# Running the conv units of a conv-plus-spectral-mix kernel from the last row blocks to the first

## The chip, the cores and the metric

The kernel runs on one core of a Trainium2 chip. The core has a matrix engine (TensorE, PE in the profile; PEld is its loading of stationary operands), a vector engine (DVE), a scalar engine (ACT), a general engine (POOL) that also issues DMAs, and a sync engine (SP) that only issues DMAs. Sixteen DMA engines move data between the device memory and the on-chip memory. The metric is the device time of one execution in microseconds (us); lower is better. Before the change the median of three runs is 177.28 us (176.27 to 177.85).

## What is computed

The input `x` is 8 batches of 3264 rows of 192 channels. First comes a causal convolution over rows with 7 taps: the 192 channels belong to 8 heads of 24, and each head has its own softmax-normalised taps. On its result `u` stands a spectral mix: the first 64 Fourier modes along the rows are taken, each mode is multiplied by its own complex 192x192 matrix, and the result is transformed back. Last comes `out = v + relu(v @ w_ch)` with `v = u + mixed`.

```python
w = softmax(weight)                       # (heads, 7)
u = einsum('hk,bskhg->bshg', w, windows(x, 7))
X = rfft(u, axis=1)[:, :64]
Y = einsum('bmd,mde->bme', X, w_r + 1j * w_i)
v = u + irfft(Y, n=S, axis=1)
out = v + maximum(v @ w_ch, 0)
```

## The kernel before

**Rows and blocks.** The rows of a batch are cut into 13 blocks of 256 rows; the last has 192. A block is held in `xall` as two halves of up to 128 rows, in bf16. Batches go in pairs: `q` is the pair (0 to 3), `i` the batch in the pair. The DMA that loads `x` casts it from four bytes to two.

**Units.** The conv stage runs over `units`: a unit is a pair and a run of blocks `(q, t0, n)`. Pair 0 has the units (0,2), (2,3), (5,4), (9,4), the other pairs (0,5), (5,4), (9,4), so there are 13 units, in rising order of blocks (L44 to L46). For each unit the four calls of `conv_group` (L295) handle two heads each. A head and a parity of the output row (`e`) have up to five products: two of the half blocks with the near part of the band matrix (L307), one for the rows that the second half of the block before gives (L312, all blocks of the unit but its first), one for those that the first half gives the second (L315), and, in units that don't begin at block 0, one of 48 columns for the first block of the unit (L319). The conv result is written over its input in `xall` (L326 on ACT for groups 0 and 2, L328 on DVE for 1 and 3), so the raw last rows of a unit are kept in a tile `side` for the next one: `keep_side` (L330) copies them on DVE (L334) before the unit starts. The products go to three PSUM tiles in turn (`zc`), so a fourth group waits until the first has been copied out.

**Fourier sums.** `dft_unit` (L336) multiplies the finished blocks of a unit with the table `ftab` and adds them up over the 13 blocks of a pair in one PSUM bank (L342). The map `after` (L376) says behind which group of which unit that is issued, one unit later in most cases. At the end of a pair the sums are copied out (L346) and `xtrans` turns them by six products a batch (L355, L357).

**The table.** `ftab` holds cosines and sines for 26 half blocks. `table_dve` (L194) computes the angles on DVE in four instructions (L198, L202, L203, L205), `table_act` (L209) the sine, the absolute value and the cosine on ACT (L213, L215, L217). Two pieces are made, half blocks 0 to 10 (`TA`) and 10 to 26; their steps are put between conv groups by the map `between` (L368).

**Loads.** All loads of `x` and of the weights are issued from POOL in program order, so that every instruction on POOL stands in one queue with them. `load_rows` (L139) loads the blocks of one batch of a unit; `load_last` (L150) loads the last block, one batch of all pairs at a time and each half by itself. The first loads of `x` have 2 and 3 blocks. Behind those of `x` come the channel matrix (L273 to L275) and the mode matrices, two loads for a group of four modes (`load_w`, L277), 16 groups in seven slots; `load_free` (L284) issues a load as soon as the group that used the slot before it has been mixed.

**Mix.** When the conv stage is over, PE alternates 12 products of a group (`mix`, L461, products L468) with transposes of `xall` and of the table (L417, L427) that the last stage needs. `mix_copy` and `mix_trans` (L474, L477) copy the products of two groups and turn them by four transposes (L481) into a bf16 PSUM tile, from which `yet_copy` (L485) copies on DVE and ACT (L491, L493). The last two groups have a path of their own (L606 to L617, transposes L608). Then the mixed modes are scaled (L435) and 52 items of the last stage (`z_c`, `z_g`, products L504) give the output, which SP stores.

The order of instructions is that in which the program writes them; each engine runs its own in that order. What is run when is thus set by hand, by `between`, `after` and the place of the loads.

Of the kernel before, what the change touches and what calls it, by code (L numbers as in the profile page):

```python
# [17 lines left out]
def kernel(  # L18
# [72 lines left out]
    side = [sb(f"side{i}", [2, D], BF16) for i in range(2)]  # L91
# [58 lines left out]
    def load_last(h):  # L150
        r = P if h == 0 else 64
        for i in range(2):
            src = bass.AP(tensor=x.tensor, offset=x.offset + (i * S + 256 * (NB - 1) + P * h) * D,
                          ap=[[D, r], [2 * S * D, NQ], [1, D]])
            nc.gpsimd.dma_start(out=xall[0:r, :, NB - 1, h, i, :], in_=src)
# [7 lines left out]
    load_rows(units[0][0], 0, *units[0][1:])  # L163
# [3 lines left out]
    load_rows(units[0][0], 1, *units[0][1:])  # L167
    load_unit(*units[1])
# [3 lines left out]
                   allow_small_or_imprecise_dtypes=True)  # L172
    load_unit(*units[2])
    load_unit(*units[3])
# [3 lines left out]
    nc.vector.memset(bandyet[:], 0.0)  # L178
    nc.vector.memset(halfpi[:], math.pi / 2)
# [56 lines left out]
    nc.vector.memset(xall[64:P, :, NB - 1, 1, :, :], 0.0)  # L236
# [26 lines left out]
    for u in units[4:7]:  # L263
        load_unit(*u)
# [6 lines left out]
    for u in units[7:]:  # L271
        load_unit(*u)
# [22 lines left out]
    def conv_group(k, g):  # L295
        q, t0, n = units[k]
        zt = zc[seq[0] % 3]
        seq[0] += 1
        sd = side[k % 2]
        for hd in range(2):  # L300
            h = 2 * g + hd
            dsl = slice(GRP * h, GRP * h + GRP)
            cols = zt[:, hd, 0:96 * n].rearrange("p (t e c) -> p t e c", t=n, e=2)
            for e in range(2):
                for half in range(2):
                    r = slice(64 * half, 64 * half + 64)
                    nc.tensor.matmul(cols[r, :, e, :].rearrange("p t (i d) -> p t i d", i=2),  # L307
                                     band[:, e, h, 0:64], xall[:, q, t0:t0 + n, half, :, dsl],
                                     start=(e == 0), stop=False, tile_position=(0, 64 * half),
                                     skip_group_check=True)  # L310
# [13 lines left out]
        srcv = zt[:, :, 0:96 * n].rearrange("p k (c d) -> p k c d", d=GRP)  # L324
        if g % 2 == 0:
            nc.scalar.copy(out=dst, in_=srcv)  # L326
        else:
            nc.vector.tensor_copy(out=dst, in_=srcv)  # L328

    def keep_side(k):  # L330
        q, t0, n = units[k]
        dst = side[(k + 1) % 2][96:P, :, :]
        if t0 + n < NB:
            nc.vector.tensor_copy(out=dst, in_=xall[96:P, q, t0 + n - 1, 1, :, :])  # L334

    def dft_unit(k):  # L336
        q, t0, n = units[k]
        xp = dftb[:, 0:2 * D]
        for t in range(t0, t0 + n):
            r = P if t < NB - 1 else LASTM  # L340
            for e in range(2):
                nc.tensor.matmul(xp, ftab[0:r, 2 * t + e, :], xall[0:r, q, t, e, :, :].rearrange("p i d -> p (i d)"),  # L342
                                 start=(t == 0 and e == 0), stop=(t == NB - 1 and e == 1),
                                 skip_group_check=True)
        if t0 + n == NB:
            nc.scalar.copy(out=xs[q % 2][:], in_=xp.rearrange("p (i d) -> p i d", i=2))  # L346
# [4 lines left out]
    def xtrans(q, i, bank):  # L351
# [12 lines left out]
        else:  # L364
            nc.scalar.copy(out=dst, in_=srcv)


    between = {(0, 0): lambda: table_act(0, TA, (0,)),  # L368
               (0, 1): lambda: table_dve(TA, NT, (0,)),
               (0, 2): lambda: table_act(0, TA, (1,)),  # L370
               (1, 0): lambda: table_act(0, TA, (2,)),
               (1, 1): lambda: table_dve(TA, NT, (1,)),
               (1, 3): lambda: table_dve(TA, NT, (2,)),
               (2, 0): lambda: table_act(TA, NT, (0,)),
               (2, 2): lambda: table_act(TA, NT, (1, 2))}
    after = {(2, 1): (0,), (2, 3): (1,)}  # L376
    after.update({(k, 1): (k - 1,) for k in range(3, len(units))})
    pend = []
    for k, u in enumerate(units):
        keep_side(k)  # L380
        for g in range(4):
# [4 lines left out]
            for j in after.get((k, g), ()):  # L386
                dft_unit(j)
                if units[j][1] + units[j][2] == NB:
                    pend = [(units[j][0], 1), (units[j][0], 0)]
# [95 lines left out]
    def yet_copy(d, t, src):  # L485
# [3 lines left out]
        srcv = src.rearrange("p g (r k) -> p (g r) k", r=4)[:, :, 0:16].rearrange("p m (c b) -> p c b m", c=2)  # L489
# [80 lines left out]
    for d in range(ND - 2):  # L570
# [8 lines left out]
        if d == 3:  # L579
# [23 lines left out]
    et2 = [ets[1][:, :].bitcast(BF16)[:, 0:2 * P].rearrange("p (g k) -> p g k", g=2),  # L603
           ets[0][:, :].bitcast(BF16)[:, 0:2 * P].rearrange("p (g k) -> p g k", g=2)]

    def last_trans(g):  # L606
        for t in range(2):
            nc.tensor.transpose(et2[t][:, g, :], ymix[d % 2][:, g, 64 * t:64 * t + P], ident[:])  # L608
# [99 lines left out]
```

## Time and profile before

The profile is of one execution of 176.96 us. Its span, from first to last instruction, is 175.1 us; 1.9 us lie around it.

| | before |
|---|---|
| median of three runs | 177.28 us (176.27 to 177.85) |
| profiled execution | 176.96 us |
| its span | 175.1 us |
| PE busy | 160.2 us, 92% |
| DVE busy | 116.2 us, 66% |
| ACT busy | 98.2 us, 56% |
| POOL busy | 51.0 us, 29% |
| read from device memory | 39.23 MB |
| written to it | 20.05 MB |

Three stretches follow each other: the conv stage to about 69 us, the mix to about 107 us, and the last stage. The row of transfer rates counts bytes on the on-chip side of the loads, which are half of those read, since loads cast to two bytes. A busy share of PE says that a product was under way, not that PE ran at its peak.

### The profile page before, as it was taken

The page shows a single profiled execution, that of the slowest core. Times are in us where ns is not written, and L with a number is a line of the kernel's source. Part 1 is how long each engine was busy: PE and PEld are TensorE (multiplying, and loading weights), DVE is VectorE, ACT ScalarE, POOL GpSimd, SP SyncE. Part 2 cuts the span into 40 slices and gives each one's busy share as a digit, 9 for nine tenths or more (in the row PEclk, how much of TensorE's full clock was granted, in tenths as well). Part 3 has the DMA queues.
Part 4 walks back from the last instruction along what each step waited for, and adds up shares of the span by engine and source line. Part 5 has one row for each costly group of instructions (what it writes and reads, how often), then busy time and mean ns, then how long its engine had stood idle before and what let it go on. Part 6 is the DMA issues. An engine that isn't in the chain of part 4 may idle for free.

```text
span 175.1 us, 7430 instructions
## 1 busy us (share of the span) xinstructions
PE 160.2 (92%) x3311; PEld 138.5 (79%) x3312; DVE 116.2 (66%) x167; ACT 98.2 (56%) x138; POOL 51.0 (29%) x82
## 2 busy tenths in 40 slices
PE   7939699999999997989999987999999999999970
PEld 2539467788888885778886974899999999999960
DVE  5797735645544554477756753888888888888880
ACT  6144565444352443467687672776667766676640
POOL 7997773614322643055534000000000000000000
PEclk9987999999999999999999999999999999999996
DMA  4999999999999999999999990299999999999995
GB/s 43 140 192 191 191 192 192 191 194 192 192 193 193 202 206 207 206 202 206 204 207 208 205 181 16 92 325 346 338 327 347 343 321 343 343 313 352 339 334 168
DMA packets 49629, 40.15 MB, mean 229 GB/s; under 512 B 28285, under 2 KB 49597, under 8 KB 49597
## 3 DMA queue, kind: packets, MB, share of 16 engines
q0 software_dynamic: 35600, 19.62, 81.1%
q1 hardware_dynamic: 13934, 20.06, 32.7%
q8 instruction: 26, 0.43, 0.9%
q14 instruction: 6, 0.05, 0.1%
q10 hardware_dynamic: 63, 0.00, 0.0%
HBM read 39.23 MB, written 20.05 MB: 339 GB/s over the span
## 4 chain that ended last, share of the span: by engine, by line
PE 78%; DMA 6%; DVE 6%; ACT 4%; issue 3%; DVEq 0%; POOL 0%; ACTq 0%; POOLq 0%
PE x_right L342 9%; PE z_right L504 9%; PE zb_left L504 8%; PE zt L504 8%; PE zs L504 8%; PE w_left L427 7%; PE x_left L307 7%; DMA arena<-in_moe_w_i_dram 6%; PE x_right L307 3%; PE w_right L468 2%; PE x_left L315 2%; PE x_left L312 2%; PE x_right L187 2%; PE w_left L417 2%; PE x_right L315 2%
## 5 line engine op out<-in xcount | busy, mean ns | idle before, releaser
L307 PEld LDWEIGHTS <-bandyet 128*64 128x64 bf16 x416 | 32.0, 114 | 9.2 <-issue 8.5
L504 PEld LDWEIGHTS <-gt 64*128 64x128 bf16 (+1 forms) x832 | 35.5, 96 | 1.7 <-issue 1.5
L307 PE MATMUL x_left<-xall,bandyet 128*64 128x192 bf16 (+3 forms) x280 | 27.8, 256 | 3.1 <-ACT xall L326 2.8
L328 DVE CAST xall<-x_left 128x768 bf16<-128x768 f32 (+3 forms) x18 | 16.8, 934 | 18.0 <-PE x_left L319 10.8
L504 PEld LDWEIGHTS <-ct 64*128 64x128 bf16 (+1 forms) x624 | 26.5, 96 | 1.0 <-DVE ct L405 0.4
L143 POOL DMA_DIRECT2D xall<-in_x_dram x26 | 22.8, 883 | 14.1 <-DMA xall<-in_x_dram 12.9
L315 PE MATMUL x_left<-xall,bandyet 128*64 128x192 bf16 (+3 forms) x140 | 26.2, 253 | 0.0
L312 PE MATMUL x_left<-xall,bandyet 128*64 128x144 bf16 (+3 forms) x140 | 25.7, 232 | 0.0
L312 PEld LDWEIGHTS <-bandyet 128*64 128x64 bf16 x208 | 23.5, 115 | 0.0
L315 PEld LDWEIGHTS <-bandyet 128*64 128x64 bf16 x208 | 23.4, 114 | 0.0
L326 ACT CAST xall<-x_left 128x768 bf16<-128x768 f32 (+3 forms) x17 | 13.9, 815 | 15.1 <-DVE side L334 8.2
L405 DVE COPY ct<-w_left 128x1024 bf16<-128x1024 bf16 x24 | 15.9, 688 | 6.9 <-PE w_left L427 4.8
L427 PE MATMUL w_left<-ident,xall 128*128 128x128 bf16 x312 | 19.6, 220 | 0.0
L342 PE MATMUL x_right<-xall,fz 128*128 128x384 bf16 (+1 forms) x104 | 19.2, 327 | 0.3 <-ACT fz L217 0.3
L427 PEld LDWEIGHTS <-xall 128*128 128x128 bf16 x312 | 17.6, 103 | 1.7
L403 ACT COPY ct<-w_left 128x1024 bf16<-128x1024 bf16 (+1 forms) x16 | 15.2, 961 | 4.2 <-PE w_left L427 3.8
L319 PE MATMUL x_left<-side,bandyet 128*64 128x48 bf16 x92 | 16.7, 190 | 0.0
L326 ACT CAST xall<-x_right 128x768 bf16<-128x768 f32 (+1 forms) x9 | 6.9, 762 | 17.4 <-PE x_right L319 8.1
L319 PEld LDWEIGHTS <-bandyet 128*64 128x64 bf16 x144 | 16.6, 115 | 0.0
L307 PE MATMUL x_right<-xall,bandyet 128*64 128x192 bf16 (+3 forms) x136 | 14.4, 254 | 1.6 <-ACT xall L326 1.6
L342 PEld LDWEIGHTS <-fz 128*128 128x128 bf16 (+1 forms) x104 | 9.1, 98 | 6.9 <-issue 0.6
L328 DVE CAST xall<-x_right 128x768 bf16<-128x768 f32 (+2 forms) x8 | 8.1, 1008 | 8.2 <-PE x_right L319 6.6
(134 smaller groups left out, 341.2 us busy)
## 6 DMA issues: line engine op xcount, KB each, us to landing
out_dram<-arena SPq DMA_DIRECT2D x25, 384.0 KB, 3.8
out_dram<-xt SPq DMA_DIRECT2D x12, 384.0 KB, 3.7
out_dram<-ct SPq DMA_DIRECT2D x10, 384.0 KB, 3.5
xall<-in_x_dram POOLq DMA_DIRECT2D x8, 384.0 KB, 14.0
xall<-in_x_dram POOLq DMA_DIRECT2D x10, 288.0 KB, 12.9
xall<-in_x_dram POOLq DMA_DIRECT2D x6, 480.0 KB, 14.6
arena<-in_moe_w_r_dram POOLq DMA_DIRECT2D x8, 288.0 KB, 9.8
arena<-in_moe_w_i_dram POOLq DMA_DIRECT2D x8, 288.0 KB, 9.8
```

The source lines that it names most:

```text
L143: nc.gpsimd.dma_start(out=dst, in_=src)
L307: nc.tensor.matmul(cols[r, :, e, :].rearrange("p t (i d) -> p t i d", i=2), band[:, e, h, 0:64], xall[:, q, t0:t0 + n, half, :, dsl], star ...
L312: nc.tensor.matmul(cols[0:64, 1:n, e, :].rearrange("p t (i d) -> p t i d", i=2), band[:, e, h, 64:P], xall[:, q, t0:t0 + n - 1, 1, :, dsl] ...
L315: nc.tensor.matmul(cols[64:P, :, e, :].rearrange("p t (i d) -> p t i d", i=2), band[:, e, h, 64:P], xall[:, q, t0:t0 + n, 0, :, dsl], star ...
L319: nc.tensor.matmul(cols[0:64, 0, e, :].rearrange("p (i d) -> p i d", i=2), band[:, e, h, 64:P], sd[:, :, dsl], start=False, stop=True, til ...
L326: nc.scalar.copy(out=dst, in_=srcv)
L328: nc.vector.tensor_copy(out=dst, in_=srcv)
L342: nc.tensor.matmul(xp, ftab[0:r, 2 * t + e, :], xall[0:r, q, t, e, :, :].rearrange("p i d -> p (i d)"), start=(t == 0 and e == 0), stop=(t ...
L403: nc.scalar.copy(out=out, in_=in_)
L405: nc.vector.tensor_copy(out=out, in_=in_)
L427: nc.tensor.transpose(tp[:, P * k:P * k + P], src, ident[:])
L504: nc.tensor.matmul(bank[0:l.shape[-1], D * e:D * e + D], l, r, start=begin, stop=end, tile_position=(64 * i, 0), skip_group_check=True)
```

## The change

Units run from the last blocks of a pair to the first: (9,4), (5,4), (0,5) for all four pairs, 12 units instead of 13. A unit's results now overwrite its blocks while the block before it still holds raw rows, so `keep_side`, the `side` tiles, their memsets and the product on `side` go; the product of L312 covers all blocks of a unit but block 0 of the pair. A unit's load covers blocks `t0 - 1` to `t0 + n - 2`, which brings the block that it needs from below; the last block is loaded by itself, for pair 0 by two short loads with both batches in one, directly behind the first two loads. These first two have 4 blocks each instead of 2.

The table is made in the three pieces 18 to 26, 10 to 18 and 0 to 10, and steps of it stand at other places; sine and absolute value of the first piece are now issued before the first unit. The first Fourier sums are issued behind groups (1,1), (2,3), (4,0) and (4,2), the later ones one unit behind as before. The memset of the unused rows of the last block moves ahead on DVE. In the mix the transposes of `ymix` become products with 64 columns of the identity (those that are used), with an f32 result, and the copies read that.

The core of the diff:

```diff
-    UNITS = ((0, 5), (5, 4), (9, 4))
-    UNITS0 = ((0, 2), (2, 3), (5, 4), (9, 4))
-    units = [(q, t0, n) for q in range(NQ) for t0, n in (UNITS if q else UNITS0)]
+    UNITS = ((9, 4), (5, 4), (0, 5))
+    units = [(q, t0, n) for q in range(NQ) for t0, n in UNITS]
...
     def load_unit(q, t0, n):
-        n = min(n, NB - 1 - t0)
+        t1 = min(t0 + n, NB - 1) if t0 + n == NB else t0 + n - 1
+        t0 = max(t0 - 1, 0)
         for i in range(2):
-            load_rows(q, i, t0, n)
+            load_rows(q, i, t0, t1 - t0)
...
+    def load_last_pair(q, h):
+        r = P if h == 0 else 64
+        src = bass.AP(tensor=x.tensor, offset=x.offset + (2 * q * S + 256 * (NB - 1) + P * h) * D,
+                      ap=[[D, r], [S * D, 2], [1, D]])
+        nc.gpsimd.dma_start(out=xall[0:r, q, NB - 1, h, :, :], in_=src)
...
-    load_rows(units[0][0], 0, *units[0][1:])
+    load_unit(*units[0])
     nc.gpsimd.memset(shift[0:KK, :], 0.0)
     nc.gpsimd.affine_select(out=shift[0:KK, :], in_=shift[0:KK, :], compare_op=ALU.not_equal, fill=1.0,
                             base=-31, pattern=[[1, 2 * PW + 31]], channel_multiplier=-1)
-    load_rows(units[0][0], 1, *units[0][1:])
-    load_unit(*units[1])
+    load_last_pair(0, 0)
+    load_last_pair(0, 1)
+    load_rows(units[1][0], 0, units[1][1] - 1, units[1][2])
...
+    load_rows(units[1][0], 1, units[1][1] - 1, units[1][2])
     load_unit(*units[2])
-    load_unit(*units[3])
...
-    for a in side:
-        nc.vector.memset(a[:], 0.0)
-    TA = 10
-    table_dve(0, TA, (0, 1, 2))
-    load_last(0)
-    load_last(1)
+    PIECES = ((18, 26), (10, 18), (0, 10))
+    table_dve(*PIECES[0], (0, 1, 2))
+    table_act(*PIECES[0], (0, 1))
+    load_last(1, NQ, 0)
+    load_last(1, NQ, 1)
+    load_unit(*units[3])
...
-                if n > 1:
-                    nc.tensor.matmul(cols[0:64, 1:n, e, :].rearrange("p t (i d) -> p t i d", i=2),
-                                     band[:, e, h, 64:P], xall[:, q, t0:t0 + n - 1, 1, :, dsl],
-                                     start=False, stop=False, tile_position=(0, 0), skip_group_check=True)
+
+                nc.tensor.matmul(cols[0:64, b0:n, e, :].rearrange("p t (i d) -> p t i d", i=2),
+                                 band[:, e, h, 64:P], xall[:, q, t0 + b0 - 1:t0 + n - 1, 1, :, dsl],
+                                 start=False, stop=True, tile_position=(0, 0), skip_group_check=True)
                 nc.tensor.matmul(cols[64:P, :, e, :].rearrange("p t (i d) -> p t i d", i=2),
                                  band[:, e, h, 64:P], xall[:, q, t0:t0 + n, 0, :, dsl],
-                                 start=False, stop=(t0 == 0), tile_position=(0, 64), skip_group_check=True)
-                if t0:
-                    nc.tensor.matmul(cols[0:64, 0, e, :].rearrange("p (i d) -> p i d", i=2),
-                                     band[:, e, h, 64:P], sd[:, :, dsl],
-                                     start=False, stop=True, tile_position=(0, 0), skip_group_check=True)
+                                 start=False, stop=True, tile_position=(0, 64), skip_group_check=True)
...
-    def keep_side(k):
-        q, t0, n = units[k]
-        dst = side[(k + 1) % 2][96:P, :, :]
-        if t0 + n < NB:
-            nc.vector.tensor_copy(out=dst, in_=xall[96:P, q, t0 + n - 1, 1, :, :])
...
+    between = {(0, 0): lambda: (table_act(*PIECES[0], (2,)), table_dve(*PIECES[1], (0,))),
+               (0, 1): lambda: table_dve(*PIECES[1], (1,)),
+               (0, 3): lambda: table_dve(*PIECES[1], (2,)),
+               (1, 0): lambda: table_act(*PIECES[1], (0,)),
+               (1, 1): lambda: table_dve(*PIECES[2], (0,)),
+               (1, 2): lambda: table_act(*PIECES[1], (1,)),
+               (1, 3): lambda: table_dve(*PIECES[2], (1,)),
+               (2, 0): lambda: table_act(*PIECES[1], (2,)),
+               (2, 1): lambda: table_dve(*PIECES[2], (2,)),
+               (2, 2): lambda: table_act(*PIECES[2], (0,)),
+               (3, 0): lambda: table_act(*PIECES[2], (1, 2))}
+    after = {(1, 1): (0,), (2, 3): (1,), (4, 0): (2,), (4, 2): (3,)}
+    after.update({(k, 1): (k - 1,) for k in range(5, len(units))})
...
+    used = ident[:, :].rearrange("p (r k) -> p r k", r=4)[:, :, 0:2 * B]
+
     def mix_trans(d):
-        et = ets[d % 2][:, :].bitcast(BF16)[:, 0:4 * P].rearrange("p (t g k) -> p t g k", t=2, g=2)
+        et = ets[d % 2][:, 0:256].rearrange("p (t g k) -> p t g k", t=2, g=2)
         for t in range(2):
             for g in range(2):
-                nc.tensor.transpose(et[:, t, g, :], ymix[d % 2][:, g, 64 * t:64 * t + P], ident[:])
+                nc.tensor.matmul(et[:, t, g, :], ymix[d % 2][:, g, 64 * t:64 * t + P], used, start=True,
+                                 stop=True, skip_group_check=True)
```

Note that `load_unit(*units[0])` now issues both batches ahead of the POOL memset and select for `shift`, where the second batch stood behind them.

More of the change, by code (lines that the diff above doesn't have):

```diff
@@ L90 @@
     ymix = [sb(f"ymix{i}", [2, D], BF16) for i in range(2)]
-    side = [sb(f"side{i}", [2, D], BF16) for i in range(2)]
     def wgroup(flat):
@@ L178 @@
     nc.vector.memset(bandyet[:], 0.0)
+    nc.vector.memset(xall[64:P, :, NB - 1, 1, :, :], 0.0)
     nc.vector.memset(halfpi[:], math.pi / 2)
@@ L235 @@
                          start=(i == 0), stop=True, tile_position=(0, 0), skip_group_check=True)
-    nc.vector.memset(xall[64:P, :, NB - 1, 1, :, :], 0.0)
     for g in range(4):
@@ L262 @@
                             base=0, pattern=[[-64, 2], [-1, 32]], channel_multiplier=1)
-    for u in units[4:7]:
+    for u in units[4:6]:
         load_unit(*u)
@@ L270 @@
                             fill=1.0, base=P, pattern=[[-1, D]], channel_multiplier=1)
-    for u in units[7:]:
+    for u in units[6:]:
         load_unit(*u)
@@ L298, in conv_group @@
         seq[0] += 1
-        sd = side[k % 2]
+        b0 = 0 if t0 else 1
         for hd in range(2):
@@ L342, in dft_unit @@
                 nc.tensor.matmul(xp, ftab[0:r, 2 * t + e, :], xall[0:r, q, t, e, :, :].rearrange("p i d -> p (i d)"),
-                                 start=(t == 0 and e == 0), stop=(t == NB - 1 and e == 1),
+                                 start=(t == UNITS[0][0] and e == 0),
+                                 stop=(t == UNITS[-1][1] - 1 and e == 1),
                                  skip_group_check=True)
-        if t0 + n == NB:
+        if t0 == 0:
             nc.scalar.copy(out=xs[q % 2][:], in_=xp.rearrange("p (i d) -> p i d", i=2))
@@ L387 @@
                 dft_unit(j)
-                if units[j][1] + units[j][2] == NB:
+                if units[j][1] == 0:
                     pend = [(units[j][0], 1), (units[j][0], 0)]
@@ L602 @@
     d = ND - 1
-    et2 = [ets[1][:, :].bitcast(BF16)[:, 0:2 * P].rearrange("p (g k) -> p g k", g=2),
-           ets[0][:, :].bitcast(BF16)[:, 0:2 * P].rearrange("p (g k) -> p g k", g=2)]
+    et2 = [ets[1 - t][:, 0:P].rearrange("p (g k) -> p g k", g=2) for t in range(2)]
     def last_trans(g):
         for t in range(2):
-            nc.tensor.transpose(et2[t][:, g, :], ymix[d % 2][:, g, 64 * t:64 * t + P], ident[:])
+            nc.tensor.matmul(et2[t][:, g, :], ymix[d % 2][:, g, 64 * t:64 * t + P], used, start=True, stop=True,
+                             skip_group_check=True)
     mix(2 * d)
```

21 lines of the change are left out of this document (5 added, 16 removed).

## The prediction

> **What bounds the kernel now.** I read the chain that ended last from its end backwards. From 106.4 us on it is PE alone, item after item of the last stage. Ahead of that stand these pieces (start, duration, what):
>
> ```profile
> 92.75 1.02 PE w_left L427 x16
> 93.77 0.26 issue
> 94.03 0.61 POOL arena L279
> 94.64 0.56 issue
> 95.22 11.15 DMA arena<-in_moe_w_i_dram
> 106.41 0.47 PE w_right L468 x10
> ```
>
> The last mode matrices land 11 us after their issue, so they did not wait for PE but stood in a full transfer queue. The DMA queue table says that this queue takes 19.62 MB, all of `x` and the weights. In one-microsecond windows (the last two columns are DMA share and GB/s) it starts badly and then never rests:
>
> ```profile
> 3.00:4.00 1.00, 1.00 (x4) 0.32 (x3) 0.59 (x4) 0.98 (x3) 1.00 (x2) 1.00 1.09 117
> 4.00:5.00 1.00, 1.00 (x13) 0.29 (x12) 0.78 (x2) 0.80 (x2) 1.00 (x3) 1.00 1.02 96
> 5.00:6.00 1.00, 1.00 (x35) 0.86 (x33) 0.17 (x2) 0.00 (x0) 1.00 (x3) 1.00 1.07 95
> 6.00:7.00 1.00, 0.95 (x5) 0.37 (x4) 0.95 (x3) 0.45 (x1) 1.00 (x2) 1.00 1.44 167
> 7.00:8.00 1.00, 0.71 (x26) 0.52 (x26) 0.90 (x4) 0.00 (x0) 1.00 (x3) 1.00 1.53 182
> 8.00:9.00 1.00, 0.73 (x34) 0.59 (x27) 0.96 (x2) 0.00 (x0) 1.00 (x2) 1.00 1.56 182
> ```
>
> From 9 us it gives 190 to 193 GB/s while `x` comes and 202 to 208 with the weights, up to 104. So the first 106 us are one transfer stream. But PE arrives only just ahead of it, as the order of PE shows (the bracket is its idle time and what ended it):
>
> ```profile
> 106.41 0.45 PE L468 MATMUL w_right<-arena,xt 128*16 128x192 bf16 x12 [0.39 <-DMA arena<-in_moe_w_i_dram]
> ```
>
> PE waits 0.39 us. Two paths end together, and a gain needs both.
>
> **The stream.** It consists of the same bytes before and after; only its start differs. POOL issues it (start, duration, count):
>
> ```profile
> 1.24 0.88 POOL L143 DMA_DIRECT2D xall<-in_x_dram  x1 [0.79 <-POOLq L692]
> 2.53 2.42 POOL L143 DMA_DIRECT2D xall<-in_x_dram  x3
> 4.93 0.32 POOL L169 IOTA ct<- 128x26 f32 x1
> 5.29 3.45 POOL L143 DMA_DIRECT2D xall<-in_x_dram  x4
> 8.70 2.78 POOL L155 DMA_DIRECT2D xall<-in_x_dram  x4
> ```
>
> An issue costs POOL about 0.85 us whether the load has 2 blocks (192 KB) or 4 (384 KB). In quarter-microsecond windows the first load ramps (31 to 77 GB/s up to 3.5 us), runs at 169 to 186 and is spent at 4.3; then the rate falls to 46 to 106 GB/s until 6.0, since the next short load is only beginning. With 384 KB the first load lasts to 5.5 us. The second is issued at 2.1 instead of 2.53, and needs about 1.6 us from issue to first byte, as the first did: it is there by 3.8. So I take the ramp as it is and 177 GB/s (mean of the last three rows above) from 3.5 to 9.0: 40 + 973 = 1,013 KB, where the six rows sum to 839 KB. The 174 KB more are **0.9 us at 191 GB/s**. From outside: if the second load brings its hole along (1.5 us at about 80 instead of 177 GB/s, 145 KB), 0.15 us are left; with 191 GB/s from 3.0 on it is 307 KB, 1.6 us. The two short loads for the last block of pair 0 (96 and 48 KB) have no equal row at the start; the nearest, the four of L155, flow at 182 to 202 GB/s in a deep queue; a hole of 145 KB at each would cost 1.5 us, so the stream could end 0.6 later than now (0.9 - 1.5). I take 0.9, because 768 KB stand ahead of them.
>
> Does the stream then stay fed? POOL's first wait for a landing comes at its fourteenth load; from there on eight loads are in flight (eight of 288 KB at 206 GB/s are 11.4 us, and the last took 11.15). After the change POOL issues fourteen loads (3.7 MB) up to about 13.5 us, then `ident` and `perm` (2.3 us, 11.39 to 13.7 now). By then some 1.9 MB are done; 1.8 MB cover those 2.3 us. Weight loads that wait for a mixed group: the first is issued at 75.94 now, with 4 us still queued (it lands 5.7 us later). PE reaches that place earlier, see below, so the cover grows.
>
> **PE's path.** From the chain I take stretches of four conv groups between two Fourier sums:
>
> ```profile
> 35.08 0.20 PE x_left L307 x2
> ...
> 38.19 1.41 PE x_right L342 x8
> 39.60 0.20 PE x_right L307 x2
> ...
> 42.68 1.41 PE x_right L342 x8
> ```
>
> 39.60 to 42.68 is two groups of 4 blocks and two of 5 (3.08 us; 25.61 to 28.69 gives the same); 35.08 to 38.19 is four of 4 blocks and six `xtrans` products (3.11); 30.10 to 33.35, with two and two and an `xtrans`, is 3.25, so an `xtrans` is 0.17. A 4-block group costs (3.11 - 0.17)/4 = 0.735, a 5-block group (3.08 - 1.47)/2 = 0.805. The 5-block group begins at block 0 and so has four products already: 912 columns for a head and parity. Four products for 768 columns are 0.805 x 768/912 = 0.68. If each product cost the same, a fifth (0.15) would go, by the columns alone nothing; I take 0.055 a group, from the 5-block row.
>
> When can PE run? The first unit (0.93 MB) is in at about 9.1 (8.5 by the rate above, plus 0.6, the lag of the first load, which landed at 5.04); the band is ready at 7.2, and 0.7 us of memset on DVE ahead of the softmax is hidden by that and by PE's warm-up up to 4.78. PE starts 1.6 us later than now (7.52). The fifth unit (4.52 MB by then) is in at about 28.0; four units with two sums need 14.3 us of PE, so 4.6 us are there for stalls. From then on everything is PE-bound: 20 groups at 0.68, 12 at 0.805, 78 sums at 0.176 (1.41/8), six `xtrans`: 13.6 + 9.7 + 13.7 + 1.0 = 38.0, **end of conv 65.9 against 69.1**. The last unit's load lands near 57, in time. What follows has the same instructions, so PE could be at the last mix at 106.0 - 3.2 = 102.8; the stream ends at 106.4 - 0.9 = 105.5 and is late. PE then waits 2.7 us more, spread over groups: weights come every 2.9 us (2 x 288 KB at 206), PE asks every 1.9 to 2.0.
>
> **At no cost.** The table is the same work in three pieces, hidden in the idle half of DVE and ACT; the side copies (nine, 0.26 us each, 0.43 of memset) free evictions that waited:
>
> ```profile
> ACT xall L326 <- DVE side L334: 15.7, 7, 4.2
> ```
>
> That wait mattered up to 24 us; now the data come last. The products in place of transposes save PE columns off the path. On it, behind the last landing, two L608 products get 64 columns less (0.05 us), and the copy reads f32: between its own row (0.28, L491) and that of L613 with 192 columns (0.36), so +0.0 to +0.08. I put both at 0. With the cover gone (PE late) the edits would show at their PE cost.
>
> **Sum.** 176.96 - 0.9 = **176.1 us**, on the scale of the profiled execution, which lies 0.3 below the median of the three runs.
>
> **Rivals.**
> *The ramp stays (0.15).* The slow start belongs to the first microseconds, not to short loads: 177.0. For it: the first load, too, crept until 3.5 us. Against: it then reached 186 alone. The Trainium skill, "DMA: Bandwidth & Descriptors", section "Anatomy of one DMA — SWDGE (gpsimd) path", gives each such DMA about 2.0 us whatever its size plus bytes at 436 GB/s, mostly completion; by that the length of the first loads would change nothing, and an estimate for 192 KB is 2.5 us, where this trace has 3.8.
> *The hole closes wholly (0.20).* 1.6 us from the stream, and perhaps some of its ragged end (104 to 106 us run at 105 and 52 GB/s): 175.0.
> *PE becomes late (0.12), slower.* On ACT the sine and absolute value of the first piece now stand ahead of the first eviction, and the three product tiles fill. Decisive is whether PE takes up the fifth unit before 31.5 us (69.5 - 38.0). If the table's 7.0 us on DVE (L198, L202, L203, L205: 2.0 + 1.3 + 1.7 + 2.0) all stall PE, it is 9.1 + 14.3 + 7.0 = 30.4; a stretch at half clock, as 11.6 to 15.0 now, adds 1.7; and if four products are no cheaper, 20 x 0.055 = 1.1 come on top: 33.2, 1.7 late, 178.7, and more where ACT's 5.6 us of table (L213, L215, L217) stall it too.
> *The clock drops in the mix (0.05).* PE stood from 8.6 to 11.57, and the granted clock is 0.50 from 11.6 to 15.0. Waits for weights of 0.9 us a group would have to add up likewise; half a 3.4 us stretch is 1.7, of which the stream hides 0.6 at the end: 177.2. Against it: 1.1 us idle at 69.1 left the clock at 1.00. In the Trainium skill, "TensorE: Matmul & The Clock Gate", section "Why this matters for your kernels", gaps above some 3 us are what to avoid; the trace agrees with its 2.9 and 1.1 us, and by that no wait in the mix would be long enough.
>
> **Numbers.** The forecast keeps 0.48; its own range is 175.0 to 176.8 (0.15 to 1.6 us, and some 0.3 between executions). With the ramp rival and part of the others the range is 174.9 to 177.9. Over 1% (1.8 us, about what a measurement here can tell from no change) faster, below 175.2: the closed hole and a little of the forecast, 0.28. Slower, from 178.7: late PE, 0.12. Between: 0.60.
>
> **What would show it.** Windows from 3 to 7 us near 180 GB/s; the last weights landing near 105.5; conv over near 66; the wait ahead of the last L468 still for that DMA. Wrong it would be if that wait were gone or the first windows looked as now.

## The result, and the profile after

The changed kernel takes 175.41 us (median of 8, 175.25 to 176.09) against 177.80 for the kernel before beside it (176.27 to 179.45): a ratio of 0.9891 (95% interval 0.9853 to 0.9930). A second set on another occasion gave 175.45 us and 0.9870 (0.9844 to 0.9897). So the change saves 1.1 to 1.3%, some 2.1 us. The forecast was 176.1 us, with 174.9 to 177.9 as its range.

The two profiled executions differ by less: 176.96 and 176.01 us, spans of 175.1 and 174.2. The first of these is among the shorter executions of its kernel, the second the second longest of its eight. That gap between profile and median turned out to be the main lesson, and the experiments are about it.

The chain that ended last, of the changed kernel (start, duration, what), still goes from PE through the last load of weights:

```profile
93.35 0.61 POOL arena L288
93.96 0.55 issue
...
94.53 11.20 DMA arena<-in_moe_w_i_dram
105.73 0.04 issue
105.77 0.47 PE w_right L470 x12
```

The landing comes at 105.7 instead of 106.4. The order of PE (in brackets, idle time and what ended it) shows mostly waits for data early, where it used to wait for ACT behind the side copies (one wait for ACT, 0.83 us at 12.5, is left), and two for weights, at group 12 and at the last:

```profile
9.31 0.43 PE L316 MATMUL x_left<-xall,bandyet 128*64 128x192 bf16 x2 [1.66 <-DMA xall<-in_x_dram]
...
18.82 0.29 PE L316 MATMUL x_right<-xall,bandyet 128*64 128x240 bf16 x2 [0.77 <-DMA xall<-in_x_dram]
...
25.27 0.27 PE L316 MATMUL x_left<-xall,bandyet 128*64 128x192 bf16 x2 [1.57 <-DMA xall<-in_x_dram]
...
97.17 0.45 PE L470 MATMUL w_right<-ct,xt 128*16 128x192 bf16 x12 [0.88 <-DMA ct<-in_moe_w_i_dram]
...
105.77 0.45 PE L470 MATMUL w_right<-arena,xt 128*16 128x192 bf16 x12 [0.58 <-DMA arena<-in_moe_w_i_dram]
```

In one-microsecond windows (last two columns: DMA share, GB/s) the stream starts later but then at once in full:

```profile
3.00:4.00 1.00, 1.00 (x4) 0.33 (x3) 0.78 (x9) 0.06 (x1) 0.92 (x4) 1.00 0.64 45
4.00:5.00 1.00, 0.69 (x2) 0.09 (x1) 0.60 (x4) 0.98 (x3) 1.00 (x3) 1.00 1.37 162
5.00:6.00 1.00, 0.84 (x34) 0.84 (x34) 0.10 (x1) 0.79 (x2) 1.00 (x2) 1.00 1.60 192
6.00:7.00 1.00, 1.00 (x13) 0.56 (x11) 0.68 (x2) 0.22 (x1) 1.00 (x3) 1.00 1.58 189
7.00:8.00 1.00, 0.59 (x2) 0.10 (x1) 0.96 (x3) 0.23 (x1) 1.00 (x3) 1.00 1.60 192
```

Summed over the packets of the queue, 1.54 MB have begun by 12 us, against 1.42 in the first profile of the kernel before; at 191 GB/s that is 0.64 us, and the last weights land 0.64 us earlier.

PE starts the fifth unit at 29.4, and its last conv product ends at 68.5 (69.1 before). It comes to the mix earlier by more than these 0.6 us, since a wait has shrunk as well. The first products behind the conv stage, before and after:

```profile
70.22 1.08 PE L417 MATMUL w_left<-ident,fz 128*64 128x128 bf16 x32 [1.12 <-DVE xall L328]
```

```profile
68.69 1.08 PE L419 MATMUL w_left<-ident,fz 128*64 128x128 bf16 x32 [0.23 <-ACT xall L331]
```

They write to the PSUM space of the two left-hand conv tiles, so they wait for the last copy out of one of these. With 13 units the 52nd and last group stands in such a tile; with 12 units the 48th stands in the third tile, on the right, and only the copy of the group before has to be over. The first mix product then starts at 74.04 instead of 75.18: of the 1.53 us up to here some 0.35 go to two more Fourier sums behind the conv stage, since the last unit now has five blocks.

### The profile page after: what moved, and what is told of

It reads as the page before. It is cut to its first block, busy times and chain, and to the rows that moved or that the text cites. A ratio compares the mean times of both kernels' runs of the same rounds, so it can differ in the third digit from the quotient of the medians.

```text
span 174.2 us, 7009 instructions
## 1 busy us (share of the span) xinstructions
PE 157.3 (90%) x3103; PEld 135.1 (78%) x3104; DVE 113.3 (65%) x158; ACT 98.4 (56%) x139; POOL 50.2 (29%) x82
## 4 chain that ended last, share of the span: by engine, by line
PE 71%; DMA 19%; POOL 4%; issue 2%; ACT 1%; DVE 1%; DVEq 0%; POOLq 0%
DMA xall<-in_x_dram 12%; PE x_right L341 9%; PE z_right L509 9%; PE zb_left L509 8%; PE zs L509 8%; PE zt L509 8%; PE w_left L429 7%; DMA arena<-in_moe_w_i_dram 6%; PE x_left L316 5%; PE x_left L321 3%; PE w_right L470 2%; PE x_right L316 2%; POOL xall L143 2%; PE w_left L419 2%; PE x_left L324 2%
## 5 line engine op out<-in xcount | busy, mean ns | idle before, releaser
L316 PEld LDWEIGHTS <-bandyet 128*64 128x64 bf16 x384 | 26.3, 110 | 11.2 <-issue 11.2
L316 PE MATMUL x_left<-xall,bandyet 128*64 128x192 bf16 (+1 forms) x256 | 25.6, 253 | 5.7 <-DMA xall<-in_x_dram 4.9
L333 DVE CAST xall<-x_left 128x768 bf16<-128x768 f32 (+1 forms) x16 | 16.1, 1007 | 18.6 <-PE x_left L324 13.3
L143 POOL DMA_DIRECT2D xall<-in_x_dram x24 | 21.6, 909 | 13.2 <-DMA xall<-in_x_dram 12.5
L331 ACT CAST xall<-x_left 128x768 bf16<-128x768 f32 (+1 forms) x16 | 13.4, 838 | 20.2 <-PE x_left L324 20.2
L324 PE MATMUL x_left<-xall,bandyet 128*64 128x192 bf16 (+1 forms) x128 | 24.4, 251 | 0.0
L321 PE MATMUL x_left<-xall,bandyet 128*64 128x192 bf16 x128 | 23.7, 246 | 0.0
L321 PEld LDWEIGHTS <-bandyet 128*64 128x64 bf16 x192 | 21.1, 110 | 0.1
L324 PEld LDWEIGHTS <-bandyet 128*64 128x64 bf16 x192 | 21.1, 110 | 0.0
L333 DVE CAST xall<-x_right 128x768 bf16<-128x768 f32 (+1 forms) x8 | 8.5, 1057 | 9.9 <-PE x_right L324 7.7
L316 PE MATMUL x_right<-xall,bandyet 128*64 128x192 bf16 (+1 forms) x128 | 13.7, 257 | 0.8 <-DMA xall<-in_x_dram 0.8
L539 ACT ACTIVATE z_right<-z_right 128x768 f32<-128x768 f32 (+1 forms) x13 | 10.3, 794 | 4.8 <-PE z_right L509 4.3
L509 PE MATMUL zb_left<-fz,gt 64*128 64x192 bf16 (+1 forms) x208 | 13.0, 243 | 0.0
L324 PE MATMUL x_right<-xall,bandyet 128*64 128x192 bf16 (+1 forms) x64 | 13.0, 256 | 0.0
```

The lines of the kernel that those rows point to most:

```text
L143: nc.gpsimd.dma_start(out=dst, in_=src)
L321: nc.tensor.matmul(cols[0:64, b0:n, e, :].rearrange("p t (i d) -> p t i d", i=2), band[:, e, h, 64:P], xall[:, q, t0 + b0 - 1:t0 + n - 1, ...
L509: nc.tensor.matmul(bank[0:l.shape[-1], D * e:D * e + D], l, r, start=begin, stop=end, tile_position=(64 * i, 0), skip_group_check=True)
L539: nc.scalar.activation(out=zt[0:m, :, 0:2 * D], in_=zt[0:m, :, 0:2 * D], func=ACT.Relu)
```

## The experiments

Two theories stood against each other at first. The *stream theory*: the loads start earlier by what the profiles show, and that is all. The *two-path theory*: in the kernel before PE is so close behind the weights that any delay of PE lengthens an execution, and the change gives it room. The ratio is always to runs of the kernel before on the same occasion. A third theory, the *short-load theory* (short loads at the head of the queue disturb the stream, and by how much differs from one execution to the next), came from the first eight runs. The changed kernel itself stood beside the first four variants only; where the others are compared with it, the medians are of different occasions, on which those of the kernel before lay within some 0.2 us of each other.

| kernel | median us | lowest to highest | ratio to before (95%) |
|---|---|---|---|
| changed, again | 175.45 | 175.12 to 175.57 | 0.9870 (0.9844 to 0.9897) |
| short first loads | 176.81 | 176.08 to 178.18 | 0.9949 (0.9923 to 0.9974) |
| five products | 175.41 | 175.18 to 175.95 | 0.9876 (0.9847 to 0.9904) |
| transposes in the mix | 175.58 | 175.47 to 175.92 | 0.9882 (0.9855 to 0.9909) |
| before, no side rows | 176.75 | 176.24 to 177.71 | 0.9958 (0.9933 to 0.9983) |
| before, long loads, first form | 186.48 | 185.88 to 187.70 | 1.0504 (1.0463 to 1.0545) |
| the same without side rows | 185.73 | 184.38 to 186.09 | 1.0446 (1.0405 to 1.0488) |
| before, PE kept busy | 177.82 | 176.51 to 178.38 | 1.0003 (0.9974 to 1.0033) |
| before, long loads, order kept | 180.46 | 179.38 to 182.00 | 1.0164 (1.0114 to 1.0214) |
| changed, PE delayed 1.5 us | 176.43 | 175.94 to 177.32 | 0.9926 (0.9893 to 0.9960) |
| before, again | 177.61 | 176.64 to 177.98 | 0.9997 (0.9969 to 1.0024) |
| changed, one short load first | 176.64 | 176.18 to 178.78 | 0.9948 (0.9917 to 0.9979) |

**The changed kernel again.** No edit.

> The changed kernel once more, beside its variants. Two theories of the gain stand against each other. Stream theory: the load stream starts earlier by what the profiles show (last weights landed 0.6 us earlier, span 0.8 us shorter), and that is the whole gain; the ratio to the kernel before should be about 0.995. Two-path theory: in the kernel before PE reaches the last mix only 0.4 us ahead of the weights, so whatever delays PE from one execution to the next lengthens it, while the changed kernel has about 1.5 us to spare; the ratio should be near 0.989 and the executions should spread over less than 1 us, those of the kernel before over 2 to 3 us.

0.9870, spread 0.45 us. The stream theory's 0.995 is out: the saving is over twice what the two profiles show. The spread is as the two-path theory said, which does not yet make its reason right.

**Short first loads in the changed kernel.**

```diff
-    load_unit(*units[0])
+    load_rows(0, 0, 8, 2)
     nc.gpsimd.memset(shift[0:KK, :], 0.0)
...
+    load_rows(0, 1, 8, 2)
+    load_rows(0, 0, 10, 2)
+    load_rows(0, 1, 10, 2)
     load_last_pair(0, 0)
```

> The changed kernel with its first unit loaded by four loads of 2 blocks, placed as the first loads before were, in place of two of 4 blocks. If the short loads make the hole in the stream, the rate falls to about 100 GB/s somewhere between 4.3 and 6 us and the last weights land about 0.6 us later than in the changed kernel, +0.6 us (ratio to the kernel before 0.992). If the slow start belongs to the first microseconds whatever the loads are, nothing changes (within 0.2 us).

1.36 us slower than the changed kernel beside it, twice what was expected. The windows show not one hole but a ragged stream up to about 13 us (four of them):

```profile
4.00:5.00 1.00, 0.54 (x2) 0.09 (x1) 0.71 (x3) 0.98 (x3) 1.00 (x3) 1.00 0.79 70
7.00:8.00 1.00, 0.81 (x4) 0.19 (x2) 0.96 (x3) 0.39 (x1) 1.00 (x3) 1.00 1.33 148
9.00:10.00 1.00, 0.00 (x0) 0.00 (x0) 0.96 (x2) 0.00 (x0) 1.00 (x3) 1.00 1.48 151
11.00:12.00 1.00, 1.00 (x18) 1.00 (x15) 0.62 (x2) 0.94 (x2) 1.00 (x2) 0.50 1.51 146
```

By 12 us 1.36 MB have begun, 0.18 MB less than in the changed kernel. PE still waits 0.89 and 0.61 us for weights at the end, and yet the executions spread over 2.1 us. So short first loads bring a spread like that of the kernel before even in the changed order. What share of the 1.36 us is theirs alone is open: six loads for the first unit are two more than the changed kernel has, each costs POOL 0.7 to 0.9 us, and since its data come later PE starts the mix at 75.6 instead of 73.8, which costs time too, as the delayed run below shows.

**Five products.**

```diff
-                nc.tensor.matmul(cols[0:64, b0:n, e, :].rearrange("p t (i d) -> p t i d", i=2),
-                                 band[:, e, h, 64:P], xall[:, q, t0 + b0 - 1:t0 + n - 1, 1, :, dsl],
-                                 start=False, stop=True, tile_position=(0, 0), skip_group_check=True)
+                nc.tensor.matmul(cols[0:64, 1:n, e, :].rearrange("p t (i d) -> p t i d", i=2),
+                                 band[:, e, h, 64:P], xall[:, q, t0:t0 + n - 1, 1, :, dsl],
+                                 start=False, stop=False, tile_position=(0, 0), skip_group_check=True)
...
+                if t0:
+                    nc.tensor.matmul(cols[0:64, 0, e, :].rearrange("p (i d) -> p i d", i=2),
+                                     band[:, e, h, 64:P], xall[:, q, t0 - 1, 1, :, dsl],
+                                     start=False, stop=True, tile_position=(0, 0), skip_group_check=True)
```

> The changed kernel with five products per head and parity again (the full-unit product cut into one for all blocks but the first and one of 48 columns). Two-path theory: a group of 4 blocks takes about 0.055 us longer, the end of conv moves by 20 x 0.055 = 1.1 us, the wait of 0.9 us for the weights of group 12 shrinks to nothing, and the time rises by 0 to 0.5 us, with a wider spread. Stream theory: no change of the time. If five products cost PE nothing, conv ends at 67.7 us as in the changed kernel.

The time is the same. In the order of PE a head and parity take 0.175 to 0.18 us instead of 0.165 to 0.17 (start to start of a product). The wait at group 12 shrinks from 0.86 us (the changed kernel beside it) to 0.44, that at the last mix stays:

```profile
96.98 0.45 PE L474 MATMUL w_right<-ct,xt 128*16 128x192 bf16 x12 [0.44 <-DMA ct<-in_moe_w_i_dram]
105.54 0.45 PE L474 MATMUL w_right<-arena,xt 128*16 128x192 bf16 x12 [0.54 <-DMA arena<-in_moe_w_i_dram]
```

The last conv product ends 0.46 us later (68.71 against 68.25). So the saving of four products is real, about 0.45 us at this place, and hidden in a wait. (The 67.7 of the expectation is the end of the last group but one; the last conv product ends at 68.5 in that profile.)

**Transposes in the mix.** `mix_trans`, `last_trans` and `yet_copy` as before the change.

> The changed kernel with the transposes of the mix as they were (128 columns into a bf16 tile). Both theories: 0 to +0.1 us, since only two of these products stand behind the last landing.

+0.13 us, near what was expected; the intervals overlap, so it could be nothing.

**The kernel before without side rows.**

```diff
-                if t0:
-                    nc.tensor.matmul(cols[0:64, 0, e, :].rearrange("p (i d) -> p i d", i=2),
-                                     band[:, e, h, 64:P], sd[:, :, dsl],
-                                     start=False, stop=True, tile_position=(0, 0), skip_group_check=True)
...
-        keep_side(k)
```

> The kernel before without the product on the kept side rows and without the copies that keep them: the rows that the last block of a unit gives the first block of the next are left out, so the convolution of 6 rows per unit is incomplete. PE's path gets shorter, the load stream stays. Two-path theory: the last weights land at 106.4 us as before, the wait ahead of the last mix grows from 0.4 to 1.5 us or more, and the median falls by about 1 us (ratio 0.993 to 0.996) with a spread under 1 us. Stream theory: ratio 1.00, spread as before.

0.75 us faster (interval 0.3 to 1.2), with a convolution that leaves those rows out. The profiled execution, the shortest of its set, shows the waits for weights that were expected:

```profile
98.02 0.45 PE L459 MATMUL w_right<-ct,xt 128*16 128x192 bf16 x12 [0.47 <-DMA ct<-in_moe_w_i_dram]
106.57 0.45 PE L459 MATMUL w_right<-arena,xt 128*16 128x192 bf16 x12 [0.43 <-DMA arena<-in_moe_w_i_dram]
```

The median fell by what the two-path theory said, but the spread stayed at 1.5 us. So PE's lateness costs something in the kernel before, though not through the last wait, where PE is ahead in the profiles of the kernel before and in this one. Through what, the delayed run below shows for the changed kernel. The wait of 1.12 us behind the conv stage is still there, since the units are still 13.

**The kernel before with long loads, first form,** and the same without side rows.

```diff
-    units = [(q, t0, n) for q in range(NQ) for t0, n in (UNITS if q else UNITS0)]
+    units = [(q, t0, n) for q in range(NQ) for t0, n in UNITS]
```

> The kernel before with all pairs cut as (0,5), (5,4), (9,4), so that its first two loads have 5 blocks instead of 2; order, side rows and five products stay. The stream should start without the hole and land about 0.6 us earlier. Stream theory: 0.6 us faster (ratio 0.9965). Two-path theory: the first unit comes in about 2.5 us later, PE becomes the one that arrives last, and the gain is lost or more: ratio 0.998 to 1.01.

> Both edits of the two runs beside it: no side rows (the same part of the computation left out) and 5 blocks in the first loads. Two-path theory: stream and PE both come earlier, and the time is that of the changed kernel to about 0.4 us (ratio 0.989 to 0.992). Stream theory: the same as the long loads alone, ratio 0.9965.

Both far slower, and neither theory had it. The edit made the fourth unit one of pair 1, whose 960 KB now stood ahead of the last block of pair 0, so that PE stood for that:

```profile
26.03 0.34 PE L307 MATMUL x_right<-xall,bandyet 128*64 128x192 bf16 x1 [7.74 <-DMA xall<-in_x_dram]
```

PE came some ten microseconds later to the mix (84.7 without side rows). In that stretch the page's row of rates falls to 18 and 0 GB/s: loads of weights wait for a mixed group, and the stream runs dry. As a test of long loads these two runs fail; as a sight of that coupling they are the clearest. They also show the wait behind the conv stage by itself: with 12 units it is 0.18 and 0.23 us in these kernels too, instead of 1.12.

**The kernel before with PE kept busy.**

```diff
             between.get((k, g), lambda: None)()
+            if (k, g) == (0, 2):
+                active(12, dftb, blank[:, 0:P], blank)
```

> The kernel before with twelve idle products of 512 columns (2.6 us at full clock) in the stretch from 8.7 to 11.6 us in which PE stands, so that its clock is not halved from 11.6 to 15.0. If the half clock delays PE's path, conv ends up to 1.7 us earlier than 69.1 and the median falls by up to 1 us; if PE waits for ACT, DVE and data there anyhow, conv ends as before and the ratio is 1.00.

The granted clock of the whole span rises from 0.982 to 0.994; the half-clock stretch from 11.6 to 15.0 us is gone:

```profile
core 0: 174.9 us, clock 0.994
```

The ratio is 1.0003, and the executions still spread over 1.9 us. PE waits for ACT up to 20.3 us in both (1.78 us here, 1.59 before), and the clock explains neither the time nor its spread.

**The kernel before with long loads, order kept.** As above, and `load_unit(*units[3])` moved behind `load_last(1)`.

> The kernel before with all pairs cut as (0,5), (5,4), (9,4), so that its first loads have 5 blocks, and with the last block's loads again ahead of the first unit of pair 1 (in the run with long loads alone that unit's 960 KB had come between, and PE stood 7.7 us for the last block). Rising order, side rows and five products stay. Short-load theory: the gain is that of the long first loads, whose lack costs more in a typical execution than in the one profiled; the stream starts as in the changed kernel (about 1.54 MB by 12 us), ratio 0.988 to 0.992, spread under 1 us. Two-path theory: PE stays close behind the weights, 0.993 to 1.0, spread of 2 us.

2.9 us slower, against both theories. The early stream is not that of the changed kernel either: the hole at 4 to 6 us is gone, but the rate falls to 130 and 142 GB/s from 6 to 8 us, and 1.42 MB have begun by 12 us, as in the first profile of the kernel before. So long first loads alone don't give the stream of the changed kernel, and the short-load theory fails here too. PE gets its first unit at 11 us, waits 2.2 us for the last block and 2.3 for the table, and ends conv at 74.0:

```profile
10.99 0.29 PE L307 MATMUL x_left<-xall,bandyet 128*64 128x240 bf16 x2 [2.43 <-DMA xall<-in_x_dram]
20.66 0.24 PE L307 MATMUL x_right<-xall,bandyet 128*64 128x192 bf16 x1 [2.24 <-DMA xall<-in_x_dram]
30.40 1.47 PE L342 MATMUL x_right<-xall,fz 128*128 128x384 bf16 x8 [2.32 <-ACT fz L216]
```

The windows show the price, with weights waiting for PE's mix:

```profile
78.00:79.00 1.00, 0.72 (x26) 0.55 (x20) 0.78 (x3) 1.00 (x2) 0.00 (x0) 1.00 0.61 110
79.00:80.00 1.00, 0.82 (x28) 0.70 (x30) 0.97 (x3) 0.33 (x1) 0.06 (x1) 1.00 0.15 21
80.00:81.00 1.00, 1.00 (x28) 0.81 (x26) 0.77 (x2) 0.54 (x1) 1.00 (x2) 1.00 0.01 1
81.00:82.00 1.00, 1.00 (x25) 0.86 (x26) 0.69 (x1) 0.57 (x3) 0.48 (x2) 1.00 0.65 66
```

Long loads put into the rising order are thus a loss; in the change the other order of work lets PE do without the early start. In the changed kernel the first Fourier sum starts at 15.1 and the second at 22.2 us, while data are awaited; here the first comes at 23.3.

**The changed kernel with PE delayed.**

```diff
             between.get((k, g), lambda: None)()
+            if (k, g) == (8, 0):
+                active(7, xtrb, blank[:, 0:P], blank)
```

> The changed kernel with seven idle products of 512 columns (1.5 us) put into PE's order behind the first group of the ninth unit. That takes the 1.4 us by which PE was ahead of the weights (0.9 at group 12, 0.6 at the last). Short-load theory: 0 to +0.2 us, spread under 1 us. Two-path theory: with PE as late as in the kernel before, the executions spread by 2 us and the median rises by 0.5 to 1 us.

1.0 us slower than the changed kernel, spread 1.4 us. The start of the stream is the same (1.54 MB by 12 us), and PE still waits at the end (0.40 and 0.55 us). The loss lies in between. POOL (the bracket again) issues the first load that needs a mixed group at 76.3 instead of 74.8:

```profile
76.33 0.61 POOL L288 DMA_DIRECT2D arena<-in_moe_w_r_dram  x1 [7.90 <-PE w_right L472]
```

and the stream thins out, where the changed kernel has 205, 220 and 204 GB/s:

```profile
77.00:78.00 1.00, 1.00 (x25) 0.76 (x23) 0.84 (x2) 0.63 (x2) 0.55 (x1) 1.00 1.04 164
78.00:79.00 1.00, 1.00 (x22) 1.00 (x20) 0.37 (x2) 0.94 (x2) 0.93 (x2) 1.00 1.06 159
81.00:82.00 1.00, 1.00 (x25) 0.77 (x23) 0.51 (x1) 1.00 (x2) 0.40 (x2) 1.00 1.14 142
```

From 57 to 90 us it moves 6.47 MB instead of 6.72; 0.245 MB at 206 GB/s are 1.2 us. So a late PE is paid through the stream, some 25 us before the last landing, and PE's wait for the last weights looks the same. The short-load theory's "0 to 0.2" is wrong here; the size is the two-path theory's, by another mechanism than it gave. The spread of 1.4 us stands beside a smooth start, so a late PE, too, can spread the executions.

**The kernel before again.** No edit.

> The kernel before once more, for a second profile of it. The first profile showed one of its shorter executions (span 175.1, while most lie at 175.2 to 176.6). Short-load theory: in a longer execution the stream has less than 1.42 MB by 12 us and the last weights land later than 106.4 us, with PE still waiting for them. Two-path theory: the stream is the same and PE is the later one, with no wait ahead of the last mix.

This profiled execution (span 176.1) is a longer one. Its early windows are ragged where the first profile's were full:

```profile
7.00:8.00 1.00, 0.98 (x39) 0.76 (x39) 0.90 (x4) 0.00 (x0) 1.00 (x3) 1.00 1.36 162
8.00:9.00 1.00, 0.49 (x21) 0.35 (x16) 0.96 (x2) 0.00 (x0) 1.00 (x2) 1.00 1.43 145
9.00:10.00 1.00, 0.00 (x0) 0.00 (x0) 0.93 (x3) 0.00 (x0) 1.00 (x2) 1.00 1.41 167
```

```profile
107.69 0.45 PE L468 MATMUL w_right<-arena,xt 128*16 128x192 bf16 x12 [0.46 <-DMA arena<-in_moe_w_i_dram]
```

1.36 MB by 12 us; the last weights land 1.3 us later than in the first profile, and PE waits for them. Of the 1.3 us some 0.6 are missing bytes (0.12 MB by 103 us, of which 0.10 by 15 us); the rest is the ragged end, where the rate falls off from 104 to 108 us instead of from 104 to 106. That is the short-load theory's picture.

**The changed kernel with one short load first.**

```diff
-    load_unit(*units[0])
+    load_rows(0, 0, 8, 2)
+    load_rows(0, 1, 8, 4)
+    load_rows(0, 0, 10, 2)
```

> The changed kernel with its first loads as 2 blocks of the first batch, 4 of the second, 2 of the first. The first rows above full rate came at 3.5 us with a first load of 2 blocks and at 4.1 us with one of 4. If the length of the very first load sets when the stream gets going and the load behind it closes the hole, the last weights land 0.3 us earlier than in the changed kernel (-0.3 us); if any short load reopens a hole, +0.3 us or more.

It was meant to beat both kernels and loses 1.2 us to the changed one. The first rows come earlier (142 GB/s from 3 to 4 us), but the stream stays ragged although a long load stands right behind the short one:

```profile
8.00:9.00 1.00, 0.00 (x0) 0.00 (x0) 0.94 (x3) 0.00 (x0) 1.00 (x2) 1.00 1.48 162
9.00:10.00 1.00, 0.00 (x0) 0.00 (x0) 0.97 (x2) 0.00 (x0) 1.00 (x2) 1.00 1.46 166
11.00:12.00 1.00, 1.00 (x28) 1.00 (x25) 0.77 (x2) 0.81 (x2) 1.00 (x2) 0.92 1.49 172
```

PE comes to the mix as early as in the changed kernel (74.13), so here the loss is that of the loads: two of 2 blocks in place of one of 4, and with them one issue of POOL more. No version beat the changed kernel.

## Why the prediction was right, and where it was not

**What bounds the kernel: right.** The load stream ends the first stretch before and after, in all four profiles of the two kernels, and PE waits for the last weights in each.

**Where the stream gains: the place right, the size wrong.** The term was 0.9 us, from one profile. In profiles it is 0.64 us by bytes at 12 us against the first execution of the kernel before (the hole closed wholly, as the second rival had it, but a first load of 4 blocks ramps longer, with 45 GB/s from 3 to 4 us instead of 117, where the ramp was taken as it was: the six windows sum to 964 KB, not 1,013) and 0.93 us against the second. In medians, short first loads cost 1.36 us in the changed kernel, and one short load 1.2 us with PE on time (first mix product at 74.13). What was missed is that the hole is a matter of the execution: the profile that the sum was made against was one of the shorter ones (176.96 us; the sets of the kernel before have medians of 177.3 to 177.8). The three executions known beforehand spread over 1.6 us, which was a sign of it. That the time still fell into the range is in part luck: the saving of 2.1 us is over twice the term, and the profiled 176.01 us meets the 176.1 of the sum only because a shorter execution of the one kernel stands against a longer one of the other.

**The ramp rival: wrong.** With the ramp alone the cause, the short loads would have changed nothing, and they cost 1.36 us. The first load landed 3.8 us after its issue with 192 KB and 5.4 with 384. By the fit of the Trainium skill ("DMA: Bandwidth & Descriptors", section "Anatomy of one DMA — SWDGE (gpsimd) path") these would be an estimated 2.5 and 2.9 us, with the fixed part by far the larger; the measurement decides, and here the size counts for more.

**PE's path: too early by 2.6 us, and too harmless.** End of conv was put at 65.9 and came at 68.5: the fifth unit started at 29.4 instead of 28.0, since the lag from stream to landing had grown from 0.6 us to about 1.5; PE's own work from there was 39.1 us without a wait, against 38.0 worked out. The conv groups make the difference, 24.4 us instead of 23.3. A 4-block group takes 0.66 to 0.68 us, as scaled from the 5-block group (0.68), but 0.76 to 0.90 in most cases where a Fourier sum follows, and a 5-block group there 1.0; and the spacing of the products in the kernel before (0.177 us for a head and parity) gives 0.71, not 0.735, so the saving is smaller. That PE was still 1.1 us earlier at the mix comes for the larger part from the wait behind the conv stage, 0.23 us instead of 1.12, which the sum did not have: it took what follows the conv stage as unchanged. The step that failed is the cover of the weight loads ("with 4 us still queued"). That was read from the landing of one load. By bytes issued and not yet begun, the queue held 0.53 MB at that issue, 2.6 us at 206 GB/s; it held 0.62 MB in the changed kernel and 0.30 MB, 1.5 us, in the delayed run. The delayed run loses 0.245 MB with the issue at 76.3; the kernel before, at 75.94, already shows 189 and 188 GB/s from 77 to 79 us, 0.035 MB or 0.2 us. PE's earlier arrival is therefore worth something by itself, which the sum put at nothing: 1.0 us in the delayed run of the changed kernel, whose PE comes to the mix as late as before (75.56 against 75.18), and 0.75 us (0.3 to 1.2) in the kernel before when the side rows are left out. How much of the 0.75 us goes through this place is not located; the bytes of two profiles (6.71 MB from 57 to 90 us without side rows, 6.68 and 6.65 before) give 0.15 to 0.3 us.

**Rivals of late PE and halved clock: did not come.** Late PE is what the long loads in rising order became (180.5 us; 178.7 had been its price). No half-clock stretch lies in the mix, and the one at 11.6 us, taken away, changed nothing.

**The free edits: right.** The copies from f32 take 0.28 us as those from bf16 did, the transposes are worth 0.1 us by the medians, within the noise, four products instead of five nothing in the time.

The parts don't add up cleanly. 1.36 (first loads) and 1.0 (PE), both measured in the changed kernel, make 2.4 us; 1.36 and the 0.75 of the kernel before make 2.1. But the short loads also made PE late, and each part was measured with the other in one state only. Which step of the change gives how much of the smooth start is open, see below.

## What to carry to other kernels

Before a sum is made against one profile, look where that execution lies among its runs: a cost that varies shows its size in the spread. Where loads wait for buffers that a late engine frees, that engine can set the end of the stream without ever being late at the end; look at the transfer rate in the middle, not only at the last wait. An edit to the start of a queue is judged with everything that needs its first pieces: long first loads gained up to 1.4 us with the right order of work behind them, and in the old order the kernel lost 2.9. And where a stage ends with a copy out of a buffer that the next one needs, count which buffer that is: one unit fewer took 0.9 us off that wait.

## What was not expected of the hardware

Long after the first load is done, and with further loads already issued, single packets take up to 1.7 us. Between 5 and 14 us a packet of 384 bytes took 0.051 us in the median of all runs. In the two executions of the kernel before 21 and 41 packets took over 0.13 us, and 37 and 16 in its variants with the same loads; with short first loads in the changed kernel 36, with one short load first 41; in the two profiles of the changed kernel none, and in three of its variants with the same first loads none, one and four.

The length of the first load is not the whole of it. The three runs of the kernel before with 5 blocks in its first loads have 32, 34 and 19 such packets, up to 1.1 us. What the smooth starts share is two loads of 4 blocks that POOL issues directly one behind the other; in the runs with 5 blocks its memset and select stood between the first two, as in the kernel before. The changed kernel with only these two instructions moved back was not run, so which of the two matters, and why, stays open.

Twelve products that kept the clock up through 11.6 to 15.0 us were worth nothing, although PE was busy there: at either clock it waits for ACT until 20.3 us, and the last conv product ends at 69.0 instead of 69.1.
